# Chunk-selected attention and a phase mixer on one core: the first pairs select alone, mask rows are copied by engines, and a new order of all instructions

## The chip, the core and the metric

The kernel runs on one core of a Trainium2 chip. The core has five engines with queues of their own: TensorE (PE, matmuls and transposes into PSUM), VectorE (DVE), ScalarE (ACT), GpSimd (POOL) and SyncE (SP, which here issues all DMAs). The metric is the device time of one execution in microseconds (us), lower is better; several runs are taken and the median is given. One execution of each kernel is also traced by the hardware profiler.

## The reference

Attention first: 4 batches, 8 heads, 768 positions, head size 64. Keys are cut into 24 chunks of 32; each query keeps the six chunks with the highest upper bound, and the causal mask applies inside them. Then a mixer over the 768 x 512 result of each batch. Cut to what matters:

```python
k_min, k_max = k_chunks.min(axis=3), k_chunks.max(axis=3)          # per chunk of 32 keys
ub = np.sum(np.maximum(q * k_min, q * k_max), axis=-1)             # [query, chunk]
ub = np.where(causal, ub, -1e9)
top_chunks = np.argsort(ub, axis=-1)[..., -6:]
scores = scale * q @ k.T;  scores = np.where(selected & causal, scores, -1e9)
x = softmax(scores) @ v                                            # -> [B, S, H*D]
# mixer
theta = x @ w_theta
y = w_tok_r @ (x * cos(theta)) + w_tok_i @ (x * sin(theta))        # over positions
u = x + y
out = u + relu(u @ w_ch)
```

## The kernel before

Every operation is recorded as a small function with its engine; a long list of numbers, `ORDER`, fixes in which order they are issued. Each engine carries out its own operations in that order and never overtakes; semaphores make it wait for what an operation needs. So the place of an operation in the list is part of the kernel. PSUM has three general buffers (`mi`), two for scores and one for attention times V.

For a pair of heads (two heads of 64 side by side fill 128 rows), k and q are loaded and transposed on TensorE. From the PSUM tile of k, DVE takes maxima and minima of chunks and ACT copies k to fp16; q goes to SBUF in fp32 and POOL casts it:

```python
def pair(b, p):
    k32 = load_heads("k", b, p); q32 = load_heads("q", b, p)
    for f in range(2):                                   # halves of 384 positions
        op("PE",  f"Tk.{b}.{p}.{f}",  ...)               # three fp32 transposes
        for j, o in ((0, ALU.max), (1, ALU.min)):
            op("DVE", f"red{j}.{b}.{p}.{f}", ...)        # km <- PSUM
        for x in range(2):
            op("ACT", f"evk.{b}.{p}.{f}.{x}", ...)       # kx (fp16) <- PSUM
    op("DVE", f"kd.{b}.{p}", ...)                        # max - min
    for f in range(2):
        op("PE",  f"Tq.{b}.{p}.{f}", ...)
        op("ACT", f"evq.{b}.{p}.{f}", ...)               # qT (fp32) <- PSUM
        for x in range(2):
            op("POOL", f"cq.{b}.{p}.{f}.{x}", ...)       # qx (fp16) <- qT
    op("DVE", f"relu.{b}.{p}", ...)                      # qr = max(qT, 0)
    v32 = load_heads("v", b, p)
    op("POOL", f"cv.{b}.{p}", ...)                       # v16 <- v32
```

Selection is done for a group of two pairs. The bound is two sets of matmuls; DVE turns it, takes the best eight of each row, compares, and turns back. The result, rows of 0 and 1 per chunk, is put under q as 24 more rows (a one-hot of -1000 under k turns them into a mask inside the score matmul). For the first group DVE copies the rows, for all others a DMA does:

```python
def group(b, g):                                         # pairs 2g and 2g+1
    op("PE", f"ub.{b}.{g}", ...)                         # 32 matmuls of 288 columns
    for x in range(2):
        # DVE: t1 (32x32 transposes), cz (memset), mx (9 x max8), lt (is_lt), t2 (transposes back)
        ...
        for pp in range(2):
            for r in range(2):
                dst = T(qx)[D:KX, QS:S].rearrange("p (i r w) -> p i r w", r=2, w=CH)[:, :, r, :]
                if b == 0 and g == 0:
                    op("DVE", ..., lambda: nc.vector.tensor_copy(out=dst, in_=T(nsT)[w0:w0 + NCH, :, :]))
                else:
                    op("SP", ..., lambda: nc.sync.dma_start(out=dst, in_=T(nsT)[w0:w0 + NCH, :, :]), dma=250)
```

A head has three score tiles (1024, 1024 and 640 columns), an exp for each on ACT, a triangle select for each on POOL, 21 matmuls with V, and a division on DVE:

```python
def head(b, h):
    for s in range(3):
        op("PE", f"sc.{b}.{h}.{s}", ...); op("ACT", f"ex.{b}.{h}.{s}", ...)
        op("POOL", f"tri.{b}.{h}.{s}", ...)              # affine_select on the diagonal blocks
    ...                                                  # av on PE, norm on DVE
```

The mixer turns x (`Tx`, copied by DVE), computes theta, sine and cosine (ACT), zi on POOL and zr on DVE, 12 matmuls of 512 columns for each of six y tiles, u on DVE. Then u is turned by columns, so that each of the four turned tiles needs all six u:

```python
    for c in range(4):
        for t in range(NT):
            nc.tensor.transpose(T(ps)[:, t * P:(t + 1) * P], T(u[t])[:, c * P:(c + 1) * P], K.ident16)
        op("PE", f"Tu.{b}.{c}", 330, [(u[t], 0) for t in range(NT)], ...)
        op("DVE", f"evu.{b}.{c}", ...)
    # then ch.{b}.{t}: four matmuls each, ot on DVE, out by DMA
```

Weights are cast on POOL, and the token weights are turned by twelve DMA transposes. Identity matrices come by DMA.

Of the kernel before, what the change touches and what calls it, by code (L numbers as in the profile page):

```python
# [9 lines left out]
FP32 = mybir.dt.float32  # L10
# [6 lines left out]
    "12|"  # L17
    "152 150 1 146 148 0 27 153 28 151 24 25 2 3 147 149 74 73 4 29 9 7 6 8 5 30 12 10 36 13 11 124 31 39 38 "
    "40 37 125 35 26 33 34 174 32 14 41 103 19 102 15 20 22 16 75 82 21 23 18 76 77 86 84 17 85 83 100 81 78 "
    "46 80 79 101 42 47 87 49 43 52 48 50 44 51 54 45 175 126 176 55 119 56 64 177 65 66 115 120 180 67 122 "  # L20
    "116 97 68 88 121 72 69 118 98 70 92 71 89 117 57 217 91 93 165 58 109 90 218 96 95 59 104 112 219 63 110 "
    "113 94 211 171 108 62 53 60 214 107 61 111 212 162 105 106 215 224 213 114 123 225 127 216 220 178 198 "
    "137 138 230 139 199 222 226 179 221 181 140 141 231 204 168 200 223 205 142 227 232 128 144 99 129 201 "
    "130 228 143 206 145 131 166 202 132 235 240 182 229 241 237 172 234 233 136 238 163 243 236 135 203 244 "
    "209 239 207 242 208 245 210 246 248 133 247 302 169 249 134 263 303 167 266 264 304 164 267 269 265 410 "
    "270 186 289 268 305 273 271 290 183 279 189 274 272 173 280 250 291 275 435 251 256 281 170 257 253 252 "
    "276 258 254 409 277 261 255 282 259 260 283 278 292 262 411 295 284 293 306 286 436 307 287 296 294 285 "
    "187 288 408 299 297 188 298 300 301 308 154 309 335 320 337 184 315 185 322 339 321 324 195 336 323 423 "
    "317 427 424 433 319 338 428 412 432 316 417 431 415 425 413 325 482 421 318 419 481 420 418 416 414 327 "
    "429 439 422 426 310 326 440 155 442 329 444 441 443 328 192 312 445 330 156 311 446 430 448 314 313 449 "  # L30
    "332 331 334 190 447 361 354 333 191 355 362 438 363 196 437 364 434 356 197 357 358 483 485 511 359 489 "
    "487 510 365 193 488 486 366 484 360 157 490 194 367 494 340 493 341 491 342 492 343 495 344 345 347 506 "
    "346 348 508 368 454 158 369 455 370 457 450 371 456 451 372 458 452 373 459 453 349 374 350 460 351 462 "
    "509 352 472 505 473 463 527 464 465 496 528 497 500 530 466 467 523 498 501 765 353 499 524 504 503 375 "
    "531 502 376 474 468 525 377 526 475 378 469 529 476 379 380 480 159 381 478 386 388 479 387 382 461 389 "
    "384 470 383 517 385 512 520 477 518 507 516 513 521 471 519 515 514 554 160 522 533 535 794 555 864 532 "
    "764 557 545 791 161 546 536 793 596 537 556 558 547 767 393 865 548 597 559 766 538 580 405 792 394 581 "
    "598 539 583 395 540 582 586 549 584 390 534 406 541 587 773 585 391 560 543 777 768 588 775 570 561 769 "
    "544 589 591 772 562 810 774 776 593 551 770 811 806 778 594 590 812 399 552 592 813 807 595 599 571 550 "
    "814 808 564 783 809 563 392 600 565 572 567 566 784 573 601 542 568 400 800 785 604 786 553 602 802 603 "  # L40
    "803 889 569 635 801 574 788 779 605 804 407 625 575 780 577 867 795 626 787 782 888 576 402 796 799 781 "
    "815 798 797 627 816 648 636 805 840 403 578 396 789 579 649 401 637 651 404 397 658 771 650 645 866 652 "
    "659 818 646 653 839 622 819 890 873 820 623 821 656 398 619 647 868 822 876 838 654 624 823 655 620 817 "
    "828 612 657 827 660 613 609 621 829 830 630 877 825 614 628 606 610 831 790 832 629 824 661 607 632 611 "
    "631 834 875 633 833 617 608 638 874 616 869 639 615 836 634 879 618 852 872 640 871 870 826 642 853 641 "
    "878 662 835 880 854 856 663 643 855 883 857 1120 644 916 882 884 1193 910 860 859 917 1194 664 887 858 "
    "837 911 665 913 918 1150 885 666 861 914 886 1123 912 686 1149 881 668 862 915 681 1121 1122 920 919 667 "
    "921 670 942 922 683 936 669 671 682 685 687 684 676 672 673 674 677 691 675 678 689 688 703 680 692 704 "
    "690 679 696 693 697 937 695 846 694 705 848 706 847 707 863 708 849 698 938 1148 709 943 939 1147 699 850 "
    "944 940 841 1139 843 1196 700 845 1195 842 941 701 844 851 947 1140 945 702 1124 1141 926 1127 1125 891 "  # L50
    "1142 1128 1126 927 955 892 710 893 901 711 956 928 902 894 712 957 1151 895 946 1154 1135 1153 1155 952 "
    "948 1221 1136 949 1220 896 953 713 1138 1143 897 714 1137 1152 950 899 1162 954 903 715 900 1156 1163 898 "
    "951 904 960 929 1160 1217 1158 1165 1166 1159 1218 905 1164 958 959 1167 1157 1245 923 930 1169 1170 909 "
    "717 1161 924 1168 908 961 1129 931 965 907 1131 718 1132 906 925 1130 966 962 1145 1134 716 932 1244 719 "
    "1219 963 1144 968 720 967 721 1133 1223 964 722 969 1222 1174 723 970 1001 1184 978 1185 1002 1186 1224 "
    "724 1246 1187 1227 725 1188 1228 1003 1007 1175 1172 726 1176 1008 1177 1190 1197 1192 727 1009 1201 1178 "
    "1004 1189 1179 728 1191 1199 1005 729 1183 1225 934 1180 1226 933 1200 1006 975 1182 1198 979 1146 1235 "
    "1181 935 1239 1171 976 730 981 980 973 971 1014 982 977 972 1015 1292 1236 983 974 1272 1240 1237 1229 "
    "1293 1243 1208 1242 1011 1231 1238 1012 1209 1010 1230 1294 1269 1233 1211 1013 1212 1273 1016 1241 1234 "
    "986 1270 1210 1266 1017 1274 984 985 1267 1271 1295 987 1173 731 1232 732 1268 1213 1018 1296 1276 1216 "  # L60
    "1214 1277 1019 1275 1215 994 1202 1297 995 1298 1203 733 1205 996 1204 734 1299 735 1207 1206 736 1300 "
    "991 737 988 992 1247 1278 989 738 993 1257 1301 1303 739 1302 1311 990 1258 1259 1308 1312 744 1304 742 "
    "1309 1313 1305 745 998 743 1306 997 1310 999 1248 1279 1000 740 1307 1280 1285 1249 1250 1020 1314 1316 "
    "1286 1281 1021 1315 1282 741 1287 1022 1317 1283 1251 755 1252 1023 1284 1260 1253 1027 1261 1254 756 "
    "1264 1288 1289 1028 757 1025 749 1263 1029 1265 1290 1024 1047 750 1030 1256 1255 1026 746 1031 751 1048 "
    "1291 1262 1049 1050 1032 747 1051 1370 748 1033 1037 1371 1034 1035 761 1038 1036 1039 1040 1073 762 1074 "
    "1041 1075 763 1066 1042 1321 1043 1076 1044 1045 1067 1322 1068 1046 1069 1070 1077 1078 1071 1323 1079 "
    "1347 1072 758 1348 1344 759 1349 1318 1345 1080 760 1052 1319 1346 1053 1054 1055 1320 1056 1057 1324 "
    "1058 1363 1325 1081 1082 1364 1326 1083 1365 1329 1327 1328 1357 1330 1084 1358 1350 1085 1351 752 1359 "
    "1086 1352 1354 753 1360 1353 1355 1361 754 1337 1356 1372 1059 1338 1373 1362 1368 1060 1339 1367 1366 "  # L70
    "1061 1369 1062 1334 1376 1335 1331 1377 1063 1332 1064 1336 1087 1065 1088 1333 1342 1340 1341 1089 1343 "
    "1090 1091 1374 1092 1375 1093 1383 1100 1385 1096 1101 1097 1094 1393 1095 1384 1387 1098 1395 1386 1378 "
    "1099 1394 1397 1102 1380 1396 1379 1114 1382 1103 1381 1117 1115 1104 1388 1116 1118 1105 1119 1390 1389 "
    "1108 1392 1106 1391 1398 1109 1107 1111 1399 1110 1400 1401 1403 1112 1402 1415 1113 1405 1416 1404 1417 "
    "1407 1418 1406 1436 1437 1438 1419 1420 1439 1421 1440 1441 1443 1442 1444 1422 1423 1445 1446 1447 1448 "
    "1424 1449 1425 1426 1427 1408 1428 1409 1410 1411 1412 1413 1429 1414 1430 1431 1432 1433 1434 1435 1454 "
    "1456 1455 1450 1457 1452 1451 1453 1458 1470 1459 1467 1460 1471 1473 1472 1468 1461 1469 1464 1462 1463 "
    "1474 1475 1465 1466 "
)

B, H, S, D = 4, 8, 768, 64
P = 128
DM = H * D
NT = S // P
CH = 32
NCH = S // CH
# [6 lines left out]
NEG = -1000.0  # L93
SEGS = [(0, 4), (1, 3), (2, 5)]
OFF = {0: 0, 4: 768, 1: 1024, 3: 1664, 2: 2048, 5: 2560}
BASE = [0, 1024, 2048]


CLASSES = {
# [50 lines left out]
def record(G):  # L150
# [325 lines left out]
    for p in range(2):  # L476
        pair(0, p)
# [166 lines left out]
```

## Time and profile before

The median of three runs is 290.14 us (290.06 to 294.89). The profiled execution has a span of 290.4 us and 5674 instructions.

| What | Value |
|---|---|
| HBM read, written | 26.16 MB, 6.29 MB |
| DMA packets | 104642, of which 98616 under 512 B |
| exp on ACT (96) | 84.0 us, 916 ns mean |
| chunk maxima and minima on DVE (64) | 33.8 us, 553 ns mean |
| q casts on POOL (64) | 34.9 us, 550 ns mean |
| triangle selects on POOL (96) | 39.3 us, 413 ns mean |
| k copies on ACT (64) | 30.1 us, 473 ns mean |
| first score matmul starts | 32.05 us |

How to read it: busy shares are averages over stages that have different limits, so the prediction cuts the span into stages. A matmul's time in the profile contains its way through the array, and neighbours overlap; the spacing of back-to-back matmuls tells what one costs. "A <- B" in the waits means that A stood idle until B released it. PEclk is the clock granted to TensorE, in tenths of full speed.

### The profile page before, as it was taken

What the parts mean: (1) busy time and instruction counts of PE and PEld (TensorE: products, weight loads), DVE (VectorE), ACT (ScalarE), POOL (GpSimd) and SP (SyncE); (2) the same over time, 40 slices, a digit from 0 to 9 for tenths busy, and PEclk for the clock granted to TensorE, in tenths of its full rate; (3) what the DMA queues carried; (4) which work ended last, traced back from release to release, by engine and by line L of the source; (5) the groups of instructions that cost most, each with busy time, mean ns of one, the idle gap of its engine ahead of it and who ended that gap; (6) DMA issues with size and microseconds to landing.
All of it is one profiled execution on the core that took longest, in us unless ns stands there. A gap on an engine that the chain in (4) does not pass through costs nothing.

```text
span 290.4 us, 5674 instructions
## 1 busy us (share of the span) xinstructions
PE 238.3 (82%) x2060; PEld 134.0 (46%) x2060; DVE 169.8 (58%) x481; ACT 163.0 (56%) x248; POOL 132.3 (46%) x246
## 2 busy tenths in 40 slices
PE   6448576788588986888799797959999999999984
PEld 2234334453234442565564444538664456544441
DVE  0334966323825596776958587765788325664253
ACT  1333467874642217788989677757796655442000
POOL 7135749342880471474679436356337222243000
PEclk9555759977999999999999999997999999999998
DMA  7699952699749626939859424720003110031005
GB/s 202 143 227 242 283 175 62 131 250 208 170 102 230 141 38 135 224 73 233 219 103 208 110 58 93 156 34 21 3 4 96 62 38 36 2 147 72 0 0 217
DMA packets 104642, 35.94 MB, mean 124 GB/s; under 512 B 98616, under 2 KB 98984, under 8 KB 104616
## 3 DMA queue, kind: packets, MB, share of 16 engines
q1 hardware_dynamic: 104616, 35.60, 55.2%
q8 instruction: 16, 0.26, 0.4%
q14 instruction: 10, 0.08, 0.1%
HBM read 26.16 MB, written 6.29 MB: 112 GB/s over the span
## 4 chain that ended last, share of the span: by engine, by line
PE 45%; DVE 25%; ACT 15%; DMA 7%; SPq 4%; issue 3%; POOL 0%; DVEq 0%; ACTq 0%; POOLq 0%
PE y L405 8%; PE y L407 8%; DVE km L187 6%; ACT pt L319 6%; PE sc L313 6%; DMA k<-in_k_dram 5%; PE ch L432 5%; ACT kx L195 5%; PE th L379 4%; PE av L343 4%; PE ub L249 4%; DVE zr L398 3%; DVE x L354 3%; DVE t L271 2%; SPq L161 2%
## 5 line engine op out<-in xcount | busy, mean ns | idle before, releaser
L319 ACT ACTIVATE pt<-sc 128x1024 f16<-128x1024 f32 (+1 forms) x96 | 84.0, 916 | 28.7 <-PE sc L313 27.9
L326 POOL TENSOR_SCALAR_AFFINE_SELECT pt<-pt 128x256 f16<-128x256 f16 x96 | 39.3, 413 | 54.8 <-ACT pt L319 52.4
L313 PE MATMUL sc<-qx,kx 88*128 88x512 f16 (+3 forms) x256 | 53.0, 321 | 12.1 <-ACT pt L319 5.5
L405 PE MATMUL y<-zr,wtokT 128*128 128x512 f16 x144 | 54.6, 379 | 1.5 <-ACT qT L214 0.5
L407 PE MATMUL y<-zi,wtokT 128*128 128x512 f16 x144 | 54.5, 379 | 1.0 <-POOL zi L394 0.9
L187 DVE TENSOR_REDUCE km<-kps 128x12 f32<-128x384 f32 x64 | 33.8, 553 | 31.3 <-ACT kx L195 26.8
L195 ACT CAST kx<-kps 64x384 f16<-64x384 f32 x64 | 30.1, 473 | 36.8 <-PE kps L182 21.2
L220 POOL CAST qx<-qT 64x384 f16<-64x384 f32 x64 | 34.9, 550 | 27.1 <-ACT qT L214 24.9
L394 POOL TENSOR_TENSOR zi<-x,sn 128x512 f16<-128x512 f16 x24 | 28.6, 1204 | 23.4 <-ACT sn L386 23.3
L313 PEld LDWEIGHTS <-kx 88*128 88x128 f16 x256 | 22.6, 101 | 33.8 <-issue 15.7
L343 PE MATMUL av<-v,pt 128*128 128x65 f16 x672 | 31.0, 198 | 4.8 <-DVE x L354 3.6
L343 PEld LDWEIGHTS <-pt 128*128 128x128 f16 x672 | 27.8, 100 | 11.6 <-ACT pt L319 3.1
L413 DVE TENSOR_TENSOR u<-y,x 128x512 f16<-128x512 f32 x24 | 16.3, 684 | 19.4 <-PE y L407 19.2
L379 PE MATMUL th<-wtheta,xT 128*128 128x512 f16 x96 | 25.6, 400 | 2.4 <-ACT kx L195 1.8
L398 DVE TENSOR_TENSOR zr<-x,cs 128x512 f16<-128x512 f16 x24 | 18.0, 761 | 14.3 <-ACT cs L390 14.2
L432 PE MATMUL ch<-wch,uT 128*128 128x512 f16 x96 | 23.7, 379 | 2.9 <-POOL wch L457 1.8
L182 PE MATMUL kps<-ident,k 128*128 128x128 f32 x96 | 18.3, 315 | 8.8 <-DMA k<-in_k_dram 4.4
L209 PE MATMUL qps<-ident,q 128*128 128x128 f32 x96 | 18.3, 318 | 7.5 <-DMA q<-in_q_dram 5.2
L214 ACT COPY qT<-qps 128x384 f32<-128x384 f32 x32 | 14.8, 481 | 16.9 <-PE qps L209 16.5
L390 ACT ACTIVATE cs<-th,pi 128x512 f16<-128x512 f32 x24 | 16.5, 698 | 12.0 <-PE th L379 11.9
L405 PEld LDWEIGHTS <-wtokT 128*128 128x128 f16 x144 | 14.0, 97 | 16.8 <-issue 2.1
L407 PEld LDWEIGHTS <-wtokT 128*128 128x128 f16 x144 | 14.1, 98 | 15.6 <-issue 2.4
(46 smaller groups left out, 265.3 us busy)
## 6 DMA issues: line engine op xcount, KB each, us to landing
k<-in_k_dram SPq DMA_DIRECT2D x32, 192.0 KB
v<-in_v_dram SPq DMA_DIRECT2D x32, 192.0 KB
q<-in_q_dram SPq DMA_DIRECT2D x32, 192.0 KB
out_dram<-ot SPq DMA_DIRECT2D x24, 256.0 KB
wtok<-in_moe_w_tok_r_dram SPq DMA_DIRECT2D x6, 384.0 KB
wtok<-in_moe_w_tok_i_dram SPq DMA_DIRECT2D x6, 384.0 KB
wth<-in_moe_w_theta_dram SPq DMA_DIRECT2D x4, 256.0 KB
wch<-in_moe_w_ch_dram SPq DMA_DIRECT2D x4, 256.0 KB
```

The source lines that it names most:

```text
L187: nc.vector.tensor_reduce(out=T(km)[:, j, 12 * f:12 * f + 12], in_=T(ps)[:, 0:384].rearrange("p (c w) -> p c w", w=CH), axis=AX.X, op=o)
L195: nc.scalar.copy(out=T(kx)[0:D, 384 * f:384 * f + 384], in_=T(ps)[x * D:(x + 1) * D, 0:384])
L220: nc.gpsimd.tensor_copy(out=T(qx)[0:D, 384 * f:384 * f + 384], in_=T(qT)[x * D:(x + 1) * D, 384 * f:384 * f + 384])
L313: nc.tensor.matmul(T(ps)[:, a0:a1], T(kx)[0:KX, j * P:(j + 1) * P], T(qx)[0:KX, q0 + a0 - o:q0 + a1 - o], start=True, stop=True)
L319: nc.scalar.activation(out=T(pt)[:, BASE[s]:BASE[s] + w], in_=T(ps)[:, 0:w], func=AF.Exp, bias=0.0, scale=SCALE)
L326: nc.gpsimd.affine_select(out=a, in_=a, pattern=[[0, 2], [1, P]], compare_op=ALU.is_ge, fill=G.zero_reg(), base=0, channel_multiplier=-1)
L343: nc.tensor.matmul(ps[:, t, :], T(pt)[:, o:o + P], T(v16)[:, j, h % 2, :], start=(j == 0), stop=(j == t))
L379: nc.tensor.matmul(T(ps), T(xT[c])[:, t * P:(t + 1) * P], K.wtheta[:, c, :], start=(c == 0), stop=(c == 3))
L394: nc.gpsimd.tensor_tensor(out=T(zi[t]), in0=T(x16)[:, t, :], in1=T(sn), op=ALU.mult)
L405: nc.tensor.matmul(T(ps), K.wtok[:, si, 0, t * P:(t + 1) * P], T(zr[si]), start=(si == 0), stop=False)
L407: nc.tensor.matmul(T(ps), K.wtok[:, si, 1, t * P:(t + 1) * P], T(zi[si]), start=False, stop=(si == NT - 1))
L432: nc.tensor.matmul(T(ps), T(uT[c])[:, t * P:(t + 1) * P], K.wch[:, c, :], start=(c == 0), stop=(c == 3))
```

## The change

Several things at once, the aim being an earlier start of the first scores, shorter ways for the mask rows, work spread over the engines, and an order of issue fitted to them:

- The first two pairs of batch 0 select alone (groups of one pair: three runs of six chunks in place of two of nine), and their k is copied from PSUM once; reductions and casts then read the SBUF copy.
- Query blocks of a group are split in contiguous runs rather than alternating blocks, and all mask rows are copied by DVE, ACT or POOL; no DMA is left there.
- In batch 0 the triangle is added to the scores by a matmul of the identity with a matrix that holds -1000 under the diagonal; in the other batches it is a select on POOL or a multiply on DVE.
- Many copies have a choice of engine, fixed by a letter in `ORDER`.
- u is turned tile by tile, so that a channel tile needs one u only.
- v of a pair comes in one DMA; identities are made on POOL; weights are loaded later; filler matmuls (`F` in `ORDER`) are put in gaps of TensorE at the start.
- The order of all operations is new.

```diff
-    "12|"
-    "152 150 1 146 148 0 27 153 28 151 24 25 2 3 147 149 74 73 4 29 9 7 6 8 5 30 12 10 36 13 11 124 31 39 38 "
...
+    "10|"
+    "6 0 8 5 51 50 7 52 53 31 97 98 15 4 9 16 10 96 20 18 F10 54 12 13 60 11 14 55 95 26 61 17 19 22 56 27 64 "
...
+    def copies(name, n, rows_full, psum, reads, writes, out, in_, order="ADP"):
+        c = {"A": ("ACT", ..., lambda: nc.scalar.copy(out=out(), in_=in_())),
+             "D": ("DVE", ..., lambda: nc.vector.tensor_copy(out=out(), in_=in_())),
+             "P": ("POOL", ..., lambda: nc.gpsimd.tensor_copy(out=out(), in_=in_()))}
+        alt(name, [c[x] for x in order], reads, writes)
...
+            if direct:
+                copies(f"evk.{b}.{p}.{f}", 384, 1, True, [(ps, 0)], [(kT, f)], ..., "AD")
+                src, rd = (lambda fs=fs: T(kT)[:, fs]), [(kT, f)]
+            else:
+                src, rd = (lambda ps=ps: T(ps)[:, 0:384]), [(ps, 0)]
...
-                        dst = T(qx)[D:KX, QS:S].rearrange("p (i r w) -> p i r w", r=2, w=CH)[:, :, r, :]
-                        eng(out=dst, in_=T(nsT)[w0:w0 + NCH, :, :])
-                    if b == 0 and g == 0:
-                        op("DVE", ...)
-                    else:
-                        op("SP", ..., lambda cp=cp: cp(nc.sync.dma_start), dma=250)
+                        eng(out=T(qx)[D:KX, x, QS + r * run:QS + (r + 1) * run],
+                            in_=T(nsT).rearrange("p i c -> p (i c)")[w0:w0 + NCH, 0:run])
+                    alt(nm, [("DVE", ..., lambda cp=cp: cp(nc.vector.tensor_copy)),
+                             ("ACT", ..., lambda cp=cp: cp(nc.scalar.copy)),
+                             ("POOL", ..., lambda cp=cp: cp(nc.gpsimd.tensor_copy))], ...)
...
+                    if on_pe:                            # batch 0
+                        nc.tensor.matmul(T(ps)[:, o:o + P], K.ident16, K.low16, start=False, stop=True,
+                                         skip_group_check=True)
...
+                if eng is nc.vector:
+                    eng.tensor_tensor(out=a, in0=a, in1=K.tri2, op=ALU.mult)
+                else:
+                    eng.affine_select(out=a, in_=a, pattern=[[0, 2], [1, P]], compare_op=ALU.is_ge, ...)
...
-            op("PE", f"Tu.{b}.{c}", 330, [(u[t], 0) for t in range(NT)], [(ps, 0)], tr)
+            op("PE", f"Tu.{b}.{t}", 220, [(u[t], 0)], [(ps, 0)], tr)
...
-    for p in range(2):
-        pair(0, p)
-    group(0, 0)
+    pair(0, 0, True)
+    group(0, (0,), True)
+    pair(0, 1, True)
+    group(0, (1,), True)
```

## The prediction

> **What bounds the kernel now.** I read the page's busy shares and slices first, to see which engine has no room and when; then a table of busy time by stage, cut where the program changes its work; then the waits; then single instructions where a stage begins or ends.
>
> ```profile
> PE 238.3 (82%) x2060; PEld 134.0 (46%) x2060; DVE 169.8 (58%) x481; ACT 163.0 (56%) x248; POOL 132.3 (46%) x246
> ...
> PE   6448576788588986888799797959999999999984
> ...
> PEclk9555759977999999999999999997999999999998
> ```
>
> TensorE is the bound, but only in the last third are its slices full; in the first quarter they are half full and the granted clock is often half. The stages, cut at the first scores (32.0), the first theta matmul (66.5), the first token-mixing matmul (81.0), batch 2's first theta matmul (214.3) and the last token-mixing matmul (277.9):
>
> ```profile
> 0.00:32.00 32.00, 17.78 (x86) 9.89 (x86) 12.03 (x36) 10.33 (x21) 15.52 (x46) 0.68 1.03 206
> 32.00:66.50 34.50, 25.71 (x294) 16.03 (x295) 18.77 (x68) 23.38 (x29) 18.64 (x37) 0.80 0.75 177
> 66.50:81.00 14.50, 10.25 (x46) 4.52 (x43) 8.77 (x17) 9.21 (x18) 8.05 (x10) 0.88 0.78 187
> 81.00:214.30 133.30, 114.33 (x1166) 67.98 (x1167) 91.24 (x291) 90.77 (x141) 70.85 (x129) 0.99 0.59 117
> 214.30:277.90 63.60, 63.10 (x428) 32.13 (x426) 32.39 (x61) 29.34 (x40) 19.23 (x25) 1.00 0.15 52
> 277.90:290.40 12.50, 7.13 (x48) 3.48 (x45) 6.60 (x11) 0.00 (x0) 0.00 (x0) 0.92 0.33 126
> ```
>
> The columns are the stretch, its length, then busy time of PE, weight loads, DVE, ACT, POOL, then clock, DMA share, GB/s. Busy PE is inflated by pipeline latency, so I price TensorE by spacing at full clock, read from back-to-back runs: 0.215 us for a 512-column matmul, 0.177 for an fp32 transpose (three in 0.53), 0.0305 for an attention-times-V matmul (21 in 0.64), 1.22 for one group of bound matmuls (32), about 0.055 for an fp16 transpose, 1.13 for a head's scores. The whole program is then 214 us of TensorE. By stage it does 8.6, 23.9, 8.4, 104.7, 61.9 and 6.5 us: 27%, 69%, 58%, 79%, 97% and about half of the time. The loss sits in the start (23 us), batch 0's attention (11), its turn to the mixer (6), the long middle (29) and the tail (6).
>
> ```profile
> 32.05 0.45 PE L313 MATMUL sc<-qx,kx 88*128 88x512 f16 x2 [2.16 <-DVE qx L289]
> ...
> 277.89 0.69 DVE L413 TENSOR_TENSOR u<-y,x 128x512 f16<-128x512 f32 x1 [1.90 <-PE y L407]
> 278.64 1.31 PEld L421 LDWEIGHTS <-u 128*128 128x128 f16 x21 [0.79 <-DVE u L413]
> ```
>
> The first scores need the selection of two whole pairs. At the end all 24 transposes of u, four copies and then all channel matmuls follow the last u. The waits and the chain of waits show what breaks the middle:
>
> ```profile
> DVE km L187 <- ACT kx L195: 26.8, 25, 9.3
> ...
> ACT kx L195 <- DVE km L187: 14.9, 21, 1.9
> ...
> PE sc L313 <- DMA qx<-nsT: 4.0, 3, 2.6
> ```
>
> ```profile
> 125.30 0.78 SPq L289
> 126.08 0.04 issue
> 126.12 2.98 DMA qx<-nsT
> ```
>
> ACT and DVE take turns on one PSUM bank of transposed k, and mask rows go by small DMAs issued one by one, 0.78 us each, with a landing behind them.
>
> **What the Trainium skill says.** "SBUF — State Buffer", section Who interferes with whom: GpSimd shares a port pair with VectorE, and a VectorE op with two SBUF inputs, or in a two-port mode, and a GpSimd op block one another. The trace agrees: zr, two fp16 SBUF inputs, runs between 411 and 1374 ns beside POOL's zi of 1142 ns.
>
> ```profile
> L398 DVE TENSOR_TENSOR zr<-x,cs x24: 411/718/1374, 69.2 to 263.1; 128x512 f16<-128x512 f16 x24
> ```
>
> "TensorE: Matmul & The Clock Gate", section What's actually happening: the clock is half after an idle window of about 3.4 us and full after a busy one. The trace agrees in outline: after PE sat idle from 5.9 to 9.0 us the mean clock from 10 to 28 us is 0.5. "DMA: Bandwidth & Descriptors", section Latency and other measured facts, gives a DMA a fixed cost of about 2 us; the chain shows 2.0 to 3.0 us for 13.5 KB mask rows.
>
> **The change, part by part.** Counts are of the instructions in both programs, durations of the rows before; an estimate is marked.
>
> TensorE: 48 mask-adding matmuls of 128 columns (48 x 0.055 = 2.6 us), and 112 filler matmuls of 128 columns in gaps of the first 40 us. Two one-pair bound groups replace one two-pair group. Sum 214 + 3 = 217 us, fillers apart.
>
> POOL loses 49 of 96 diagonal selects (24 to TensorE, 25 to DVE as a multiply; 49 x 0.41 = 20 us), 64 half-width q copies (34.9) for 12 whole and 4 half ones (13.6, estimate), 15 of 24 zi, 14 casts; it gains 24 mask-row copies (0.4 each, estimate), 7 zr, 8 relus, 9 small subtractions and 7 k copies. 132 falls to about 92 us.
>
> ACT gains 15 mask-row copies (4.5), 14 q copies (10), 7 relus (4), 21 copies of xT and uT (12), 4 kT copies and 6 casts (6); it loses 24 k and 10 q evacuations (34 x 0.475 = 16). 163 rises to about 184 us.
>
> DVE gains 17 k and 10 q evacuations (13), 6 q copies and 8 casts (7), 25 multiplies (6), 15 zi (8), 21 more mask copies (2); it loses 15 relus, 9 subtractions, 7 zr, 13 of the xT and uT copies (26 together), and some port waits. 170 rises to about 180 us.
>
> SP loses 56 mask-row DMAs (56 x 0.78 = 44 us of issue) and 16 v loads.
>
> On the path, by stage:
> - Start. Weights no longer go first, the identity is made on POOL, and pair 0 selects alone. Pair 0 and 1's k and q are eight loads of 192 KB; at 206 GB/s (first stage) to 227 (a fuller slice of the page), with 0.54 us to issue one, the last lands near 9.5 us. DVE then has eight reductions (4.4 us, now from SBUF, no turns with ACT), ending near 11; subtract, the small bound group (near 13), then shorter transposes, six instead of nine maxima a head, compare, transpose back: about 4 us; mask copies and a head start for clock: scores near 19 instead of 32, 13 us earlier.
> - Batch 0's attention. Here ACT sets the pace: my count gives 31.8 us of ACT work from first scores to first theta before, done in 34.5. Now it is 34.6 us. At about 90% it takes 38.5: first theta near 57.5, 9 us ahead.
> - Theta to mixing: 5.1 us TensorE, 7.8 DVE: about 10 us, mixing from 67.5 (13.5 ahead).
> - Middle, to batch 2's first theta: TensorE 113 (the new order puts more of batch 3 here), ACT 104, DVE 103. The old efficiency was 79%. The mask DMAs (4.0 us of visible PE waits plus the broken chains around them), the wait of channel matmuls on all u, and part of the port waits go; but ACT and DVE now have 92% of TensorE's load. I choose 86%: 131 us, to 198.5.
> - End: 64 us of TensorE, of which 3 after the last mixing matmul; 61 at 97% is 63, then u 0.7, two transposes, two or three channel tiles, ot 0.7 and the output's 3.2 us: 7 instead of 12.5. Sum 268.5.
>
> **The rivals.** First, the middle is bound by three balanced in-order engines: with 79% as before, 143 us, the end is 281. For it: ACT and DVE both rise by 10 to 20 us, and no engine overtakes its own queue, so a late copy on ACT holds the next exp. Against: mask rows no longer pass through SP, whose every step is visible in the chain, and half of the selects leave POOL. Second, the start is supply-bound: DMA share is already 1.03 in the first 32 us, and if q loads land late or the mask copies queue behind casts on ACT and POOL, scores start at 25 and the total is near 274. Third, late weights: token weights are now loaded after batch 1's first q and k, and the mixer of batch 0 could wait for the DMA transposes; 5 to 8 us, some 275. Fourth, all gains carry and the middle reaches 92%: 123 us, total 260.
>
> **Range and chances.** The middle's efficiency moves the total by 1.5 us per percent, and the start by up to 6. From 82% with a late start to 92%: 257 to 282. To be within 2% of 290.1 the total must exceed 284.3, which needs middle and start both to fail; an order made for wrong durations could do so. Faster 0.88, within 2% 0.07, slower 0.05.
>
> **What would show it.** First score matmul between 17 and 22 us; first theta near 57; batch 2's theta near 198; under 8 us from last mixing matmul to end; no DMA wait before scores; zr nearer 411 ns; ACT over 180 us and POOL under 100. It is wrong if the first score comes after 25 us, if scores wait for ACT or POOL copies of mask rows, if y waits on a DMA transpose, or if PE's busy share of the middle stays at 86%.

## The result, and the profile after

The changed kernel takes 252.15 us (median, 251.2 to 254.31) where the kernel before, timed beside it, takes 291.58 (290.06 to 294.89). The ratio is 0.867, with a 95% interval of 0.858 to 0.877: faster by 13%. The prediction was 268.5 us with a range of 257 to 282. The direction was right; the gain is nearly twice what was put, and the time lies below the range.

From the page of the changed kernel, the busy time of each engine, and TensorE's slices with its clock:

```profile
PE 230.7 (92%) x2234; PEld 139.0 (55%) x2234; DVE 186.3 (74%) x563; ACT 184.2 (73%) x281; POOL 101.5 (40%) x172
...
PE   7989878779599999999999989999998999999993
...
PEclk9999999979889999999999999999999999999999
```

ACT and DVE do more than before, and TensorE runs 174 matmuls more in less busy time, its mean clock being 0.986 instead of 0.926; all of it in 40 us less. TensorE's slices are full from the twelfth, not only in the last third, and the clock is at 90% or more in all but three slices. The same stages as in the prediction, cut at the same events; columns as there: stretch, length, busy PE, weight loads, DVE, ACT, POOL, clock, DMA share, GB/s:

```profile
0.00:19.10 19.10, 16.32 (x186) 11.51 (x186) 11.96 (x53) 10.50 (x21) 13.01 (x40) 1.00 1.08 195
19.10:56.20 37.10, 30.37 (x425) 22.10 (x424) 28.27 (x88) 33.78 (x49) 17.26 (x26) 0.96 1.15 251
56.20:62.40 6.20, 5.76 (x33) 2.42 (x26) 6.01 (x32) 4.71 (x9) 2.48 (x3) 0.96 1.27 222
62.40:180.40 118.00, 112.75 (x1131) 69.32 (x1129) 100.44 (x293) 101.21 (x155) 54.58 (x90) 0.99 0.68 148
180.40:244.10 63.70, 62.65 (x463) 32.53 (x456) 37.06 (x97) 32.81 (x47) 14.19 (x16) 1.00 0.09 34
244.10:250.70 6.60, 2.81 (x16) 1.13 (x14) 2.58 (x4) 1.17 (x2) 0.00 (x0) 1.00 0.41 159
```

Beside the prediction's steps, in us of the profiled executions (290.4 and 250.7):

| Stage | before | put | after | miss |
|---|---|---|---|---|
| start, to the first scores | 32.0 | 19 | 19.1 | 0 |
| batch 0's attention, to the first theta | 34.5 | 38.5 | 37.1 | -1.4 |
| theta to the first token mixing | 14.5 | 10 | 6.2 | -3.8 |
| middle, to batch 2's first theta | 133.0 | 131 | 118.0 | **-13.0** |
| end, to the last mixing matmul | 63.8 | 63 | 63.5 | 0.5 |
| tail | 12.5 | 7 | 6.8 | -0.2 |

Start and tail were right to 0.2 us. In the timeline (start, length, engine and line, operation, tiles, and in brackets the idle time ahead and who ended it), the first score matmul, the last u and the first transpose of it:

```profile
19.14 0.38 PE L357 MATMUL sc<-qx,kx 88*128 88x512 f16 x1
...
243.91 0.69 DVE L470 TENSOR_TENSOR u<-y,x 128x512 f16<-128x512 f32 x1 [0.39 <-PE y L464]
...
244.66 0.35 PEld L478 LDWEIGHTS <-u 128*128 128x128 f16 x4 [0.19 <-DVE u L470]
```

After the last u only four transposes are loaded where there were 21. The miss is the middle. Its TensorE work, 113 us by the prediction's prices, is done in 118.0: 96% where I chose 86. (At the same prices the old middle stood at 83%, not at the 79% of the prediction; the part on why it was right and wrong works this out.) The waits (who waited for whom: us in total, times, longest) name almost nothing of what stood there before:

```profile
PE sc L357 <- DVE qx L325: 3.3, 3, 1.6
...
DVE km L221 <- ACT kx L164: 1.6, 3, 0.7
```

DVE's wait for ACT on the bank of transposed k was 26.8 us and is 1.6. Scores wait for no DMA. Cut at batch 1's first theta matmul, the middle of the kernel before reads

```profile
81.06:148.74 67.68, 56.36 (x552) 32.80 (x553) 45.44 (x148) 40.34 (x65) 35.28 (x65) 1.00 0.73 148
148.74:214.10 65.36, 57.77 (x615) 35.05 (x613) 45.54 (x144) 50.39 (x76) 35.45 (x65) 0.97 0.45 86
```

and that of the changed kernel

```profile
62.39:117.31 54.92, 51.75 (x509) 32.07 (x508) 45.95 (x134) 45.45 (x69) 29.89 (x51) 0.97 1.05 210
117.31:180.41 63.10, 61.01 (x626) 37.27 (x623) 54.51 (x159) 55.78 (x87) 24.70 (x40) 1.00 0.36 94
```

12.8 of the 15 us saved lie in the first half, where batch 1's attention runs beside batch 0's mixing. Part of that is work that the new order does elsewhere: TensorE has 509 matmuls there instead of 552, and 626 instead of 615 in the second half. TensorE's idle time, the length less its busy time, falls by 8.1 us in the first half (11.3 to 3.2) and by 5.5 in the second (7.6 to 2.1). In the first half about the same DVE time and more ACT time are packed into 13 us less.

### The profile page after: what moved, and what is told of

It reads as the page before. It is cut to its first block, busy times and chain, and to the rows that moved or that the text cites. A ratio compares the mean times of both kernels' runs of the same rounds, so it can differ in the third digit from the quotient of the medians.

```text
span 250.7 us, 5951 instructions
## 1 busy us (share of the span) xinstructions
PE 230.7 (92%) x2234; PEld 139.0 (55%) x2234; DVE 186.3 (74%) x563; ACT 184.2 (73%) x281; POOL 101.5 (40%) x172
## 4 chain that ended last, share of the span: by engine, by line
PE 64%; DVE 14%; DMA 8%; ACT 5%; POOL 3%; issue 2%; SPq 2%; ACTq 0%
PE sc L357 11%; PE y L462 11%; PE y L464 11%; PE ch L486 7%; PE av L398 5%; DMA k<-in_k_dram 4%; PE ub L280 4%; DMA q<-in_q_dram 4%; PE qps L197 3%; PE kps L197 3%; DVE zr L452 3%; PE th L437 3%; DVE zi L452 2%; ACT pt L367 2%; POOL qr L248 2%
## 5 line engine op out<-in xcount | busy, mean ns | idle before, releaser
L377 POOL TENSOR_SCALAR_AFFINE_SELECT pt<-pt 128x256 f16<-128x256 f16 x47 | 20.0, 427 | 47.5 <-ACT pt L367 47.1
L221 DVE TENSOR_REDUCE km<-kps 128x12 f32<-128x384 f32 x56 | 29.1, 548 | 5.2 <-PE kps L197 3.3
L470 DVE TENSOR_TENSOR u<-y,x 128x512 f16<-128x512 f32 x24 | 16.5, 687 | 12.8 <-PE y L464 12.8
L437 PE MATMUL th<-wtheta,xT 128*128 128x512 f16 x96 | 23.7, 381 | 0.8 <-ACT sn L444 0.7
L492 DVE SCALAR_TENSOR_TENSOR ot<-ch,u 128x512 f32<-128x512 f32 x24 | 16.5, 688 | 8.2 <-PE ch L486 8.0
L420 ACT COPY uT<-ups 128x512 f16<-128x512 f16 x15 | 8.8, 585 | 18.5 <-PE ups L478 18.3
L164 ACT CAST kx<-kps 64x384 f16<-64x384 f32 x40 | 18.7, 473 | 1.7 <-PE kps L197 0.9
L409 DVE TENSOR_TENSOR x<-av,rec 128x384 f16<-128x384 f32 x32 | 17.8, 558 | 1.1
L452 POOL TENSOR_TENSOR zr<-x,cs 128x512 f16<-128x512 f16 x7 | 8.4, 1203 | 24.3 <-ACT cs L448 24.3
L197 PE MATMUL kps<-ident,k 128*128 128x128 f32 x96 | 15.6, 282 | 2.1 <-DMA k<-in_k_dram 1.2
L452 POOL TENSOR_TENSOR zi<-x,sn 128x512 f16<-128x512 f16 x9 | 11.2, 1250 | 14.1 <-ACT sn L444 14.1
```

The costliest lines, as they stand in the source:

```text
L164: c = {"A": ("ACT", int(n * 0.833 + 60), 0, lambda: nc.scalar.copy(out=out(), in_=in_())), "D": ("DVE", int(n / 0.96 + 70) if psum else in ...
L197: nc.tensor.transpose(T(ps)[:, i * P:(i + 1) * P], T(src)[:, 3 * f + i, :, :].rearrange("p x d -> p (x d)"), K.ident32)
L221: nc.vector.tensor_reduce(out=T(km)[:, j, 12 * f:12 * f + 12], in_=src().rearrange("p (c w) -> p c w", w=CH), axis=AX.X, op=o)
L377: eng.affine_select(out=a, in_=a, pattern=[[0, 2], [1, P]], compare_op=ALU.is_ge, fill=G.zero_reg(), base=0, channel_multiplier=-1)
L437: nc.tensor.matmul(T(ps), T(xT[c])[:, t * P:(t + 1) * P], K.wtheta[:, c, :], start=(c == 0), stop=(c == 3))
L452: eng.tensor_tensor(out=T(dst), in0=T(x16)[:, t, :], in1=T(src), op=ALU.mult)
```

## The experiments

Four readings of the middle were open: the mask rows no longer pass through SP and its DMAs; the work is spread over the engines; the order of issue is new; or the start gives TensorE a clock that it then keeps (the fillers). The last can't carry the middle, whose mean clock was 0.99 before as it is now; its run is under The start. All kernels below compute the whole reference. Ratios are to the kernel before, timed beside each. A letter behind a number in `ORDER` picks the engine of an operation (none, b, c: its first, second, third choice).

### Mask rows and engines, one by one and together

**Mask rows by DMA again (a_maskdma).** In the changed kernel the 56 mask-row copies of the two-pair groups go by SP, at the same places in the order.

```diff
+                    if n == 2:
+                        op("SP", nm, 450, [(nsT, 0)], [(qx, ("m", x, r))], lambda cp=cp: cp(nc.sync.dma_start), dma=250)
+                        continue
```

> The changed kernel, with the mask rows of all groups of two pairs (56 copies) sent by DMA from SP again, at the same places of the order. The middle of the changed kernel (first token mixing to batch 2's first theta) took 118.0 us for 113 us of TensorE work, 96%, where I had put 86%. Theory A (the mask-row DMAs were what held the old middle back): at least 12 us come back, total 264 or more, and TensorE's waits in the middle end on the DMA of qx. Theory B (spreading the copies over engines did it): under 5 us, total below 257. Theory C (the order itself, fitted to true durations, did it): 3 to 8 us, as the order was made without these DMAs.

**The old engines (a_oldengines).** 152 operations go back to the engine of the kernel before. The mask rows stay on engines, and the order is untouched.

```diff
-    ... 21 63c 75c F16 33 66 32 73b ...
+    ... 21 63c 75 F16 33 66 32 73 ...
```

> The changed kernel in its own order, with every choice of engine set back to that of the kernel before (k copies on ACT, q casts, v and weight casts, selects and zi on POOL, relu, subtraction, xT, uT and zr on DVE); mask rows stay copied by engines as in the changed kernel. Theory A (mask DMAs): total within 4 us of the changed kernel, below 256. Theory B (spread of work): the middle falls back toward 80 to 86%, total 264 or more, with waits of TensorE for POOL or ACT. Theory C (order): 255 to 262.

**Both (a_oldengines_maskdma).** Both edits: the changed kernel's order with, in the main, the operations of the kernel before.

> Both at once: old engines and mask rows by DMA, in the new order, new start, new u tiles. Theory C (the order itself carries the middle): total at most 262 and the middle under 127 us. Theories A and B together: the middle is back at 133 to 140 us and the total at 268 to 275. If it is over 275, the order is a worse one for these operations than the old order was.

Measured, as total (ratio and interval) and the middle in the profile:

| | spread engines | old engines |
|---|---|---|
| mask rows on engines | 252.15 (0.867), middle 118.0 | 264.31 (0.914, 0.907 to 0.921), middle 128.8 |
| mask rows by DMA | 288.64 (0.997, 0.994 to 1.001), middle 140.4 | 299.02 (1.034, 1.026 to 1.043), middle 148.5 |

Mask rows by DMA cost 36.5 us with the spread engines and 34.7 with the old ones; the old engines cost 12.2 and 10.4. In this order the two parts add up. With neither of them the new order is slower than the kernel before. Sending these 56 small copies by DMA again takes away the whole gain. The waits and the middle of a_maskdma show how:

```profile
PE sc L360 <- DMA qx<-nsT: 31.8, 13, 8.2
```

```profile
73.17:213.52 140.35, 118.52 (x1132) 72.06 (x1130) 94.07 (x276) 98.45 (x147) 49.09 (x76) 0.91 0.54 124
```

Scores wait 31.8 us for a DMA (20.6 of them in the middle), up to 8.2 us at once, and the clock of the middle falls from 0.99 to 0.91: the same matmuls are busy for 118.5 instead of 112.75 us, so some 6 of the 22 us lost in the middle are matmuls at a lower clock. This goes with the waits: each of the seven stretches of this trace at half clock begins during such a wait or within 0.6 us of its end. Another 11 us go in batch 0's attention (48.1 against 37.1). The chain of waits of a_maskdma from a turned-back mask to the next scores (start, length, what; SPq is SP issuing):

```profile
71.84 0.83 DVE nsT L317 x2
...
74.56 0.75 SPq L325
75.31 0.05 issue
75.36 0.71 SPq L325
...
77.44 2.36 DMA qx<-nsT
79.80 0.05 issue
79.85 1.57 PE sc L360 x5
```

7.2 us lie between the end of the turn-back (72.67) and the scores (79.85): issues in a row, two of them for loads, and then the landing. An engine's copy of the same rows takes 0.23 us on DVE and 0.42 or 0.43 on POOL and ACT (medians). In the kernel before, scores waited 4.0 us for these DMAs in all. Its order has other work between a mask and its scores: from the end of a turn-back to the first scores that read it there are at least 4.9 to 10.0 us in its seven groups with DMAs (the shortest of each group in the trace), and 0.9 to 3.5 us in the same groups of the changed kernel.

In a_oldengines the middle is

```profile
61.55:190.34 128.79, 115.33 (x1132) 69.54 (x1130) 98.30 (x271) 93.67 (x148) 72.33 (x123) 0.97 0.62 136
```

ACT and DVE have less work than in the changed kernel (93.67 against 101.21, 98.30 against 100.44), POOL more, and TensorE is held up more: 88% by the same count. Its longest waits are those of scores for mask copies on DVE, 7.2 us in the whole run where the changed kernel has 3.3. So the load on ACT and DVE, on which I set 86%, was not what limits the middle.

**Half of the mask rows by DMA (a_maskdma_half).** Only the second run of each head's rows goes by SP, 28 copies.

```diff
+                    if n == 2 and r == 1:
+                        op("SP", nm, 450, [(nsT, 0)], [(qx, ("m", x, r))], lambda cp=cp: cp(nc.sync.dma_start), dma=250)
+                        continue
```

> The changed kernel with only the second run of each head's mask rows (28 of 56) by DMA, the first run by engines as in it. If the cost is the landing time (2.4 us seen, the same for one DMA as for two), most of the 36 us come back: total 276 or more. If it is SP's issue (0.72 us each, in a row), half or less: 262 to 270.

272.75 us, 0.938 (0.929 to 0.947). Half of the DMAs cost 20.6 of the 36.5 us, 56%. The longest wait falls from 8.2 to 6.3 us: both the row of issues, which halves, and the landing, which stays, have a part.

### The same ideas in the old order

**All mask rows on DVE in the kernel before (b_maskdve)**

```diff
-                    if b == 0 and g == 0:
+                    if True:
```

> The kernel before, in its own order, with all 64 mask-row copies on DVE (294 ns each, 56 x 0.29 = 16 us more DVE) in place of 56 DMAs. This is the reverse of the run in which the changed kernel gets the DMAs back and loses 36 us. If the DMAs cost the old kernel as much as that (theory A at full size), it gains 20 us or more: 270 or less. If the old order, made for late mask rows, hides most of them (theory C: the cost of the DMAs depends on the order), it gains the 6 us of TensorE waits on them and a little more: 280 to 288.

304.06 us, 1.045 (1.035 to 1.055): 12 us slower, which neither reading had expected. Its waits:

```profile
PE av L343 <- DVE x L354: 7.7, 8, 2.3
...
PE ups L421 <- DVE u L413: 5.9, 2, 5.3
```

The copies put 16.0 us on DVE in the middle (107.0 against 91.0, 40 copies more: 0.40 us each with what they hold up), ahead of the divisions and of u, and TensorE waits longer for those (3.6 and 1.9 us before).

**The same 56 copies on POOL and ACT (b_maskpoolact)**

```diff
-                    if b == 0 and g == 0:
+                    if b or g:
+                        e = "POOL" if r else "ACT"
+                        op(e, ..., lambda cp=cp, r=r: cp(nc.gpsimd.tensor_copy if r else nc.scalar.copy))
+                    elif b == 0 and g == 0:
```

> The kernel before with its 56 mask-row DMAs as copies, half on POOL and half on ACT (DVE, as the fullest of the queues in the middle, had lost 12 us by taking them). If DVE's own load was the reason of that loss: 282 to 290 here, faster than before. If any engine copy at these places of the old order holds its queue (it then waits for nsT in order): 293 or more.

297.81 us (293.47 to 298.92) against 289.6 (288.58 to 295.6) beside it. No interval comes of these runs: its four lie at 293.5 and above, five of the seven beside it at 288.6 to 289.7 and two at 295 and above. Slower is likely but not shown; a gain is not seen, and the middle, 133.5 us, is that of the kernel before (133.0). In both runs the rows keep the alternating blocks of the kernel before. In the old order, then, the operation that is worth 36 us in the new one is worth nothing on the engines tried.

**The old order in the changed kernel (a_oldorder).** Its own order to the first theta; from there the operations stand in the order of the kernel before, with some 70 places moved where no buffer was free or an input was missing. The turns of u, now one per tile, take the places of the turns by column.

> The changed kernel's operations and engines throughout, its own order up to batch 0's first theta, and from there the order of the kernel before (about 60 of some 1,100 places moved where a buffer would not be free; u tiles turned where the columns were). Theory C (the order must fit the durations): the middle goes from 118 back to 128 us or more, total 262 or more. Theories A and B (the operations as such made the middle): middle under 123 us, total under 257.

320.45 us, 1.108 (1.104 to 1.112). Part of this is the joint of the two orders: between 55 and 72 us TensorE is busy for 7.8 of 17.6 us, and it stays thin to about 130. So I compare the stretch from batch 1's first theta to the last mixing matmul, which starts 90 us behind the joint. In the profile of a_oldorder it is

```profile
161.85:231.40 69.55, 57.74 (x616) 35.36 (x614) 49.56 (x168) 54.69 (x83) 26.40 (x43) 0.98 0.28 59
231.40:304.49 73.09, 65.00 (x428) 32.40 (x428) 35.00 (x76) 32.34 (x45) 14.18 (x16) 1.00 0.12 44
```

142.6 us, against 126.6 in the changed kernel and 129.2 in the kernel before. No one wait of TensorE carries it: the largest in that stretch are matmuls with V for exp (3.0 us) and theta for the turned u (1.8). New operations in the old order are slower than either kernel, as old operations in the new order are: what gains is the fit of one to the other.

### What of the engine spread counts

**k copies back on ACT (a_kact).** 16 copies of transposed k out of PSUM go from DVE back to ACT.

```diff
-    ... 101b 77 141 105 ... 166 130b 86c ... 124b 164 ...
+    ... 101 77 141 105 ... 166 130 86c ... 124 164 ...
```

> The changed kernel with all k copies on ACT, as before (16 moved from DVE, 16 x 0.47 us more for ACT, 8.8 us less for DVE). Setting all engines back had cost 12 us. If the spread of k copies was the larger part of that: 257 or more. If the queue that is behind is DVE's (waits for mask copies on DVE were the longest there): within 2 us of 252, or faster.

256.01 us, 0.878 (0.871 to 0.886), 255.5 to 256.72 where the changed kernel had 251.2 to 254.31; the middle is 122.0 us. DVE's wait for ACT on this bank comes back in part:

```profile
DVE km L221 <- ACT kx L164: 11.6, 11, 2.7
```

3.9 us, a third of what the old engines cost in all, and between the two expectations. It can't be told apart from the next run's cause: with these copies on ACT, nine k tiles are read by ACT and DVE in alternation where five were.

**Readers in turns (a_turns).** In the changed kernel the four readers of a k tile in PSUM (two copies, maximum, minimum) mostly stand grouped by engine. Here those of 19 tiles alternate; engines, places and work stay.

```diff
-    "48b 100 89 41c 39b 108 47b 114 107 F17 228 226 101b 77 ..."
+    "48b 101b 89 41c 39b 108 47b 114 105 F17 228 226 100 77 ..."
```

> The changed kernel with the readers of 19 of its k tiles alternating between DVE and ACT as in the kernel before, at the same places, engines and work unchanged. If turns are costly: 255 or more. If not: within 2 us of 252.

256.88 us (256.11 to 259.03), 0.881 (0.872 to 0.889): 4.7 us more. Its waits on this bank (in the changed kernel 1.6 and 0.3 us):

```profile
DVE km L221 <- ACT kx L164: 5.2, 9, 1.1
...
ACT kx L164 <- DVE km L221: 5.1, 11, 1.1
```

"PSUM — Partial Sum Buffer", section Specifications (TRN2), of the Trainium skill quotes that ScalarE and VectorE can read PSUM in parallel as long as there is no bank collision. A k tile is one bank, and the trace agrees so far as each engine waits there until the other is done.

**The reverse in the kernel before (b_redfirst).** There 22 of 32 k tiles alternate fully. Both reductions now come ahead of both copies, at the same places.

```diff
-    "... 74 73 4 29 9 7 6 8 5 30 12 10 36 13 11 ..."
+    "... 74 73 4 29 9 6 5 7 8 30 10 11 36 12 13 ..."
```

> The kernel before, with the four readers of each k tile in the order reduction, reduction, copy, copy at the same four places of its order; nothing else is changed. If the turns between ACT and DVE held the old middle: DVE's and ACT's waits on each other (26.8 and 14.9 us) fall by half or more, and the total falls by 4 us or more, to 286 or less. If they only filled time in which both had to wait anyway: within 2 us of 290 to 292.

288.32 us, 0.989 (0.985 to 0.993): 3.3 us gained, between the two expectations; the middle is 130.4. DVE's wait for ACT on this bank, 26.8 us, is gone, and in the table stand

```profile
ACT kx L195 <- DVE km L187: 27.5, 15, 7.0
...
DVE km L187 <- PE kps L182: 20.3, 15, 8.0
```

where ACT had waited 14.9 us and DVE 4.2 for the transposes. So most of the 27 us did not leave the table: ACT waits 12.6 us more, and DVE now waits 16.1 us more for TensorE. What it was worth is 3 us of time.

**The relus of POOL on DVE (a_reludve).** Eight letters change (`425b` to `425` and so on).

> The changed kernel with its eight relus of POOL on DVE: 1681 ns each on POOL, 459 on DVE. POOL has room (40% busy), but a relu there may hold DVE's copies that share its port (mask copies take 201 to 1192 ns). If that holds up the way to the scores: 1 to 3 us faster. If not: DVE gets 3.7 us more and the total rises by 0 to 2.

251.03 us (248.8 to 252.52), 0.862 (0.851 to 0.874). Not told apart from the changed kernel.

**The triangle of batch 0 as a select (a_tripool).** 24 selects on POOL in batch 0 in place of 48 matmuls, each right behind its exp.

```diff
-TRI_PE = (0,)
+TRI_PE = ()
```

> The changed kernel with batch 0's triangle as 24 selects on POOL in place of 48 matmuls. TensorE loses 2.6 us of work before the first theta, POOL gains 10. ACT sets the pace there (33.8 busy of 37.1 us), so I expect little: first theta between 55 and 57.5 us, total within 1.5 us of the changed kernel. If the select was the longest link from exp to V, as the change suggests, first theta comes 1.5 us or more later.

256.84 us, 0.881 (0.868 to 0.894). Batch 0's attention is 2.0 us longer, not within the 1.5 us expected, though the trace has 47 matmuls fewer there:

```profile
19.10:58.18 39.08, 31.24 (x378) 21.17 (x377) 27.91 (x88) 33.71 (x49) 26.62 (x50) 0.88 1.07 237
```

ACT's work is the same (33.7), and the clock is 0.88 instead of 0.96. The select is one more link between exp and the matmuls with V, where a matmul ahead of exp has no hand-over; whether that link or the clock makes the 2.0 us is not shown. The middle is 2.4 us longer too (120.4).

### The start

**No fillers (a_nofill).** The 112 filler matmuls go.

```diff
-    ... 10 96 20 18 F10 54 12 13 60 ...
+    ... 10 96 20 18 54 12 13 60 ...
```

> The changed kernel without the 112 filler matmuls in the gaps of the start (the ten at the very start stay). I had not counted on the clock: in the changed kernel it is full from 0 to about 53 us, in the kernel before it was half for about 31 us of the first 60. If the fillers hold it: half clock for 10 us or more in the first 40, first theta 2 to 5 us later than 56.2 us, total 254 to 258. If the denser real work holds it: clock and total as with them (251 to 253).

250.71 us (250.3 to 250.91), 0.866 (0.860 to 0.872): nothing lost. The first 40 us, of the kernel before, then of a_nofill:

```profile
0.00:40.00 40.00, 23.28 (x127) 12.82 (x135) 18.34 (x59) 15.57 (x29) 20.06 (x54) 0.65 1.00 221
```

```profile
0.00:40.00 40.00, 29.87 (x321) 19.35 (x321) 31.05 (x121) 30.43 (x50) 24.28 (x57) 0.96 1.12 223
```

Denser real work holds the clock; the fillers (then 1.00) add nothing that reaches the end.

**Pair 0 wholly first (a_pair0first).** No fillers, and the loads, transposes, reductions and selection of pair 0 stand ahead of all of pair 1.

```diff
-    "6 0 8 5 51 50 7 52 53 31 97 98 15 4 9 16 10 96 20 18 F10 54 12 13 60 ..."
+    "6 5 8 7 0 51 50 52 53 31 97 98 15 9 16 10 20 13 18 12 96 95 26 27 22 ..."
```

> The changed kernel without fillers, with the first part reordered so that pair 0 goes through transposes, reductions and selection wholly ahead of pair 1 (loads too). First scores at 13 to 15 us instead of 18.9. ACT is the pace of batch 0's attention (91% busy), so only part remains: first theta 1 to 4 us earlier than 54.2, total 247 to 250 against 250.7 without fillers.

253.61 us, 0.878 (0.874 to 0.882). The first scores come at 13.35 instead of 18.9 us, but the first theta at 56.8 instead of 54.2:

```profile
0.00:13.35 13.35, 8.73 (x59) 4.90 (x59) 6.19 (x34) 5.86 (x12) 8.23 (x31) 1.00 1.10 189
13.35:56.80 43.45, 33.74 (x440) 24.02 (x440) 33.52 (x107) 38.80 (x59) 22.18 (x33) 0.92 1.10 235
```

ACT does 5.86 + 38.80 = 44.7 us before the first theta, as it does in a_nofill, and pair 1's copies now stand between the exps. An earlier first score is worth nothing where ACT's sum sets the next event.

**No fillers and relus on DVE (a_nofill_reludve).** Both edits.

> The changed kernel without fillers and with POOL's eight relus on DVE: each alone gave about 1 us less than the changed kernel (250.7 and 251.0 against 252). If they add up: 249.5 to 250.5.

250.59 us (250.44 to 251.25), 0.867 (0.864 to 0.869). Of the edits tried none beats the changed kernel beyond the interval of the ratios.

## Why the prediction was right in direction and too small

- **Start, "scores near 19 instead of 32": right**, at 19.14, and the tail's 7 us too (6.8). The loads, eight reductions and a small bound group came as counted: the reductions end at 11.2 us ("near 11"), pair 0's bound at 13.0 ("near 13"). The second rival, a late start, and the third, a mixer that waits for its weights, fell: scores start on time, and mixing waits for no transpose.
- **Batch 0's attention, 38.5: 37.1.** ACT sets the pace as put: 33.8 us of its work in 37.1, 91%, for 90 chosen. The triangle by TensorE is worth about 2 us of it (a_tripool), its clock included. Of the old stage the prediction counted too much: 31.8 us of ACT work where its own table has ACT busy for 23.4, and 23.9 us of TensorE where the 294 matmuls of that stage make 17.8 at its prices. Only the new count of ACT, 34.6, went into the forecast, and that was right.
- **Theta to mixing, "about 10 us": mis-sized, 6.2.** The step took DVE's 7.8 us of work and added margin. DVE has 6.0 us there and is busy for all but 0.2. The step zr is cheaper than before where POOL does not stand in the way:

```profile
L452 DVE TENSOR_TENSOR zr<-x,cs x17: 408/424/1379, 59.2 to 223.1; 128x512 f16<-128x512 f16 x17
```

  Behind the count stand shortest, median and longest in ns; the median was 718 before and is now 424. In both traces every zr of DVE that took over 430 ns overlaps an operation of POOL.
- **Middle, "I choose 86%: 131 us": the step that failed**, by 13 of the 18 us of all stages. The sum of 113 us of TensorE work came as put, and so did the loads of ACT (101 for 104) and DVE (100 for 103). Two things failed in the share.
  The first is its base. At the prediction's own prices the old middle's matmuls in the trace (20 heads' scores, 399 with V, 192 of 512 columns, 126 fp32 and 96 fp16 transposes, six groups of bounds) make 111 us and not 104.7; the 6 us were counted into batch 0's attention. So the old middle stood at 83%, not 79, and the same seven points more would have given 90% and 126 us.
  The second, and the larger, is the reason for no more than that: that ACT and DVE at "92% of TensorE's load" keep in-order engines from it. At these loads the middle reached 96% and 118.0 us; with less on both it reached 88% (a_oldengines). What a full engine costs depends on whether its queue brings each operation when it is needed. I took the old middle's share as the property of such a program, gave it a few points for the waits that go, and gave the new order itself nothing but a risk.
- **The price of an fp32 transpose, 0.177 us, was wrong**, which moves the shares but hardly their ratio. It is a group of three, 0.53 us, divided by three, and so holds the last one's way through the array. In a_reludve, at full clock, six in a row and three:

```profile
10.51 0.85 PE L197 MATMUL qps<-ident,q 128*128 128x128 f32 x6
...
15.64 0.55 PE L197 MATMUL qps<-ident,q 128*128 128x128 f32 x3
```

  Three more cost 0.30 us, and in the traces the matmul behind such a transpose starts 0.11 us after it. With 0.11 the old and the new middle hold 102 and 105 us of TensorE work, 77% and 89% of their time: the gain is the same, but more is left to gain than 96% says.
- **The mask rows were put at their visible cost**, "4.0 us of visible PE waits plus the broken chains". In the old order that is about right, even too much (b_maskdve, b_maskpoolact). In the new order they are worth 36 us, because it places scores right behind their masks. The first rival, 79%, was wrong for the same reason; the fourth, 92% and 260 us, was nearest, and its share still too low. One of the prediction's signs of being wrong showed faintly: scores wait 1.0 us, once, for a mask copy on POOL.
- **The engine sums**: ACT 184 as put, DVE 186 for 180, POOL 101 for 92. POOL's eight relus, to which the prediction gives no price, are 13 us of it at 1.64 each.
- **Named in the prediction but not priced**: the clock. From 0.65 to 1.00 over the first 40 us, it comes with the denser start, and it is lost again where scores wait (0.91 in a_maskdma).

What stays open: why the old middle leaves TensorE idle for some 13 us more than the new one has no single cause that these runs show. Readers in turns are a part (2.6 us of the old middle in b_redfirst). In its first half, a late load of k (4.4 us in the chain of that half, 6.5%) and the mask DMAs (3.0 us, 4.4%) are only seen in the trace; the DMAs could not be taken out of the old order without a loss, and the load was not tested. The turns of u by tile, the contiguous mask rows and the single load of v are in all runs with the new operations, and none was taken back alone. That the new order stands or falls with the short mask path is shown; that a better order for the old operations does not exist is not.

## What to carry to other kernels

The efficiency of a stage under in-order engines belongs to an order and its durations together, so neither the idle share of the old order nor the busy share of the engines says what a new order can reach; price the stage at the bound engine's work and let the range reach up to what the best stage of the same kernel already shows (here 97%). Read a small matmul's price from how far apart starts lie in a long row, not from the length of a short group. A step on a short per-head chain should be valued by its latency where the order leans on it, not by the waits it shows in an order that hides it. And a wait that goes from the table may only have moved: 26.8 us of DVE's went, ACT's and DVE's other waits took most of it, and the time fell by 3.3.

## What the runs showed of the hardware that I had not expected

- The same relu, 128x576 fp32 into SBUF, by engine in the changed kernel (shortest, median, longest in ns):

```profile
L248 POOL TENSOR_SCALAR qr<-qT x8: 1635/1644/1949, 35.1 to 176.4; 128x576 f32<-128x576 f32 x8
L250 ACT ACTIVATE qr<-qT x7: 682/686/716, 10.2 to 114.2; 128x576 f32<-128x576 f32 x7
L248 DVE TENSOR_SCALAR qr<-qT x1: 459/459/459, 156.7 to 156.7; 128x576 f32<-128x576 f32 x1
```

  POOL takes 3.6 times DVE's time. "GPSIMD Engine Reference", section Performance versus the Vector engine, of the Trainium skill speaks of the same arithmetic throughput, for DVE at 1x, and of 1.96 times for a large fp32 addition; for this operation the measured ratio is nearly twice that. It costs nothing here, as a_reludve shows: POOL has the room.
- A small copy within SBUF costs 0.71 to 0.75 us of SP's issue as a DMA and lands 2.4 us after the start of that issue (chain of a_maskdma), against 0.23 to 0.43 us on an engine, but a DVE copy of mask rows takes up to 1.19 us at worst.
- Transposes alone held TensorE's full clock in a_nofill. Its trace has a record of the clock from 5.6 us on, and the clock is full from there to 19.3 us; from 6.0 to 11.3 us TensorE ran nothing but 24 fp32 transposes of q and k, and was busy for 3.4 us. (The ten opening matmuls before them took 634 ns each, by the median, where later ones of that size take 379, so the 1.00 that the views give for the first 5.6 us is not to be relied on.) In the kernel before, after 3.1 us of idle time, the same transposes ran at half clock. "TensorE: Matmul & The Clock Gate", Part 4, PE-mode transpose, says that such transposes don't bring the full clock; whether those of this kernel are of that mode the trace doesn't tell, but here they did not lose it.
